# Issuing k^T v of two pairs of heads in one run, from the third batch on

## The chip, the cores and the metric

The kernel runs on one core of a Trainium2 chip. Its time is the device time of that core in microseconds (us), the median of several executions. Engines are written as in the profile: PE is TensorE's matmuls, PEld its weight loads, DVE VectorE, ACT ScalarE, POOL GpSimd, SP the engine that issues the transfers.

## The reference

```python
def _attn_ref(q, k, v, g_norm):            # (8, 8, 576, 64): batch, heads, sequence, head size
    kv = np.einsum('bhsd,bhse->bhde', k, v)
    out = np.einsum('bhsd,bhde->bhse', q, kv)
    rms = np.sqrt(np.mean(out * out, axis=-1, keepdims=True) + 1e-06)
    return out / rms * g_norm
def _moe_ref(x, w_gate, w_val, w_out):     # x: (4608, 512), w_gate and w_val: (512, 1536)
    gate = 1.0 / (1.0 + np.exp(-(x @ w_gate)))
    return gate * (x @ w_val) @ w_out
```

Linear attention without a softmax, normalised per head, and behind it a gated feed-forward layer over 4608 rows (casts, and the reshaping between the two, are left out above). The kernel computes in fp32; the weights come in 8 bytes an element and are converted in the start-up. The feed-forward layer is most of the work.

## The kernel before

The rows are handled in chunks of 512. The first two batches of attention are computed up front. The feed-forward layers of the first rows are done by *plain* matmuls, the rest by seven products of blocks in place of eight (p1 to p7 below). From the third batch on attention is a filler: each pair of heads is a list of steps, and one step goes out at each *slot*, a place between matmuls of the feed-forward layers. The steps of a pair are (cut; the 12 calls of `matmul` below show in the trace as 24 instructions, each of which I call a pass):

```python
def kv_mm():        # k^T v: 24 passes on TensorE, in two halves of the output's partitions
    d["kv"] = ps = at_ps("kv")
    for j in range(NJ):
        js = slice(HD * j, HD * j + HD)
        for e in range(2):
            nc.tensor.matmul(ps[HD * e:HD * e + HD, 0, 0:HD], pairs[n]["k"][:, e, js], pairs[n]["v"][:, e, js],
                             start=(j == 0), stop=(j == NJ - 1))
def kv_out():       # VectorE copies the two 64 x 64 blocks out
    ...
# q_mm transposes of q, q_out ScalarE copy to qT, u_mm q k^T v, u_square ScalarE, u_sum VectorE,
# u_root ScalarE, u_norm VectorE (L268, L270), x_mm transposes, x_out ScalarE copy (L288)
    return [kv_mm, kv_out, q_mm, q_out, u_mm, u_square, u_sum, u_root, u_norm, x_mm, x_out]
```

All four results on PSUM, where matmuls put their results (k^T v, transposed q, u, transposed x) take the same single buffer, "at":

```python
def at_ps(kind):
    return psum_at.tile([P, 2, 512], FP32, tag="at", name="at")
```

A block of the first layer on a chunk has seven pairs of products, each with one slot behind it; the sums of `h_sums` follow at its end:

```python
for i, (p, r) in enumerate(zip(one[0], two[0])):   # p1, p6, p2, p7, p5, p4, p3
    p()
    r()
    slot()
    ...
one[1]()
two[1]()
h_sums(c, f)
```

Six such blocks (slots 0 to 41) and a second layer with 28 more slots make one steady batch of 123.4 us.

Of the kernel before, what the change touches and what calls it, by code (L numbers as in the profile page):

```python
# [10 lines left out]
FP32 = mybir.dt.float32  # L11
# [12 lines left out]
def kernel(  # L24
# [13 lines left out]
    B, H, S, HD = q.shape  # L38
# [3 lines left out]
    NHP = H // 2  # L42
    NJ = 6
    NP = S // NJ
# [9 lines left out]
    sb = ctx.enter_context(tc.tile_pool(name="sb", bufs=2))  # L54
# [6 lines left out]
    first = first_ctx.__enter__()  # L61


    NE = 2 * NHP
    pairs = {n: {} for n in range(B * NHP)}

    def ahead(n):
        return (n + 4,) if n + 4 < NE else (NE,) if n + 1 == NE else () if n < NE else (n + 1,)

    def load_kv(n):  # L70
        if n >= B * NHP:
            return
        b, h0 = n // NHP, 2 * (n % NHP)
        for name, src in (("k", k), ("v", v)):
            t = (first if n < NE else sb).tile([NP, 2, NJ * HD], FP32, tag=name, name=name, bufs=4 if n < NE else 1)
            nc.sync.dma_start(out=t, in_=src[b, h0:h0 + 2].rearrange("h (p j) d -> p h (j d)", j=NJ))
            pairs[n][name] = t

    def load_q(n):
        if n >= B * NHP:  # L80
            return
        b, h0 = n // NHP, 2 * (n % NHP)
        t = (first if n < NE else sb).tile([NP, NJ, 2, HD], FP32, tag="q", name="q", bufs=4 if n < NE else 1)
        for e in range(2):
            nc.sync.dma_start(out=t[:, :, e, :], in_=q[b, h0 + e].rearrange("(p j) d -> p j d", j=NJ))
        pairs[n]["q"] = t
# [98 lines left out]
    for n in range(4):  # L185
        load_kv(n)
        load_q(n)
        if n == 0:
            load_next_unit()
# [18 lines left out]
    def chunk(c):  # L208
        if c not in xT:
            xT[c] = sb.tile([P, NMT, G], FP32, tag="xT", name="xT", bufs=3)  # L210
        return xT[c]

    def attention(n, at_ps):

        b, m = divmod(n, NHP)
        d = {}

        def kv_mm():
# [7 lines that stand above are left out]
        def kv_out():  # L226
            for e in range(2):
                es = slice(HD * e, HD * e + HD)
                nc.vector.tensor_copy(out=kvs[n % 2][es, es], in_=d["kv"][es, 0, 0:HD])
            for i in ahead(n):  # L230
                load_kv(i)

        def q_mm():
            d["q"] = ps = at_ps("q")
            for j in range(NJ):
                c0 = NP * (j % JH)
                nc.tensor.transpose(ps[:, j // JH, c0:c0 + NP], pairs[n]["q"][:, j].rearrange("p e d -> p (e d)"),  # L237
                                    ident[0:NP, 0:NP])

        def q_out():  # L240
            d["qT"] = sb.tile([P, 2, JH * NP], FP32, tag="qT", name="qT")
            nc.scalar.copy(out=d["qT"], in_=d["q"][:, :, 0:JH * NP])
            for i in ahead(n):
                load_q(i)

        def u_mm():

            ps = at_ps("u")
            d["u"] = ps[0:NP, :, 0:JH * P]
            for j in range(NJ):  # L250
                c0 = P * (j % JH)
                nc.tensor.matmul(ps[0:NP, j // JH, c0:c0 + P], d["qT"][:, j // JH, NP * (j % JH):NP * (j % JH) + NP],  # L252
                                 kvs[n % 2], start=True, stop=True)

        def u_square():
            d["sq"] = sb.tile([NP, 2, JH * P], FP32, tag="sq", name="sq")
            nc.scalar.activation(out=d["sq"], in_=d["u"], func=AF.Square)

        def u_sum():
            d["ms"] = sb.tile([NP, 2, 2 * JH], FP32, tag="ms", name="ms")  # L260
            nc.vector.tensor_reduce(out=d["ms"].rearrange("p i n -> p (i n)"),  # L261
                                    in_=d["sq"].rearrange("p i (n d) -> p (i n) d", d=HD), axis=AX.X, op=ALU.add)

        def u_root():
            nc.scalar.activation(out=d["ms"], in_=d["ms"], func=AF.Sqrt, bias=eps[0:NP], scale=1.0 / HD)

        def u_norm():
            nc.vector.reciprocal(d["ms"], d["ms"])  # L268
            d["xn"] = d["sq"]
            nc.vector.tensor_tensor(out=d["xn"].rearrange("p i (n d) -> p i n d", d=HD),  # L270
                                    in0=d["u"].rearrange("p i (n d) -> p i n d", d=HD),
                                    in1=d["ms"].unsqueeze(3).to_broadcast([NP, 2, 2 * JH, HD]), op=ALU.mult)

        def x_mm():
            d["x"] = ps = at_ps("x")
            for j in range(NJ):
                c0 = NP * (j % JH)
                nc.tensor.transpose(ps[:, j // JH, c0:c0 + NP], d["xn"][:, j // JH, P * (j % JH):P * (j % JH) + P],  # L278
                                    ident[0:NP, 0:NP])

        def x_out():

            s0 = 0
            while s0 < S:
                c, o = divmod(S * b + s0, G)
                i, r = divmod(s0, S // 2)
                n_ = min(G - o, S // 2 - r)
                nc.scalar.activation(out=chunk(c)[:, m, o:o + n_], in_=d["x"][:, i, r:r + n_], func=AF.Copy, scale=g_col)  # L288
                s0 += n_

        return [kv_mm, kv_out, q_mm, q_out, u_mm, u_square, u_sum, u_root, u_norm, x_mm, x_out]


    fill = deque()
# [3 lines left out]
            fill.popleft()()  # L298

    def feed(b, at_ps):  # L300
        for n in range(NHP * b, NHP * b + NHP):
            steps = attention(n, at_ps)

            fill.extend(steps[:-2] + [lambda: None] * 2 + steps[-2:])

    def flush():
        while fill:
# [27 lines left out]
    def at_ps(kind):  # L335
        return psum_at.tile([P, 2, 512], FP32, tag="at", name="at")
# [51 lines left out]
    late = deque()  # L388
# [230 lines left out]
    t2w[1] = b12  # L619
    tt(out=t2w[3], in0=b22, in1=b12, op=ALU.subtract)  # L620
    feed(2, at_ps)
    second_layer(0)
    for n in (1, 2, 3, 4):
# [19 lines left out]
    for c in range(2, NG):  # L643
        if c + 1 < B:
            feed(c + 1, at_ps)
        first_layer_fast(c)
        sums_of(c + 1)
        second_layer_fast(c)
        flush()
# [30 lines left out]
```

## Time and profile before

| | before |
|---|---|
| time, median of 3 | 1146.07 us (1144.22 to 1146.63) |
| profiled span | 1143.9 us |
| PE busy | 1118.9 us, 98% |
| chain that ended last | PE 93% |
| first plain matmul of the feed-forward layer starts | 45.80 us |
| from there to the first k^T v run of the steady part | 261.41 us |
| a steady batch | 123.38 us, five of them |

I call what lies ahead of the first plain matmul the start-up, the stretch from there to the first k^T v run of the steady part the mixed part (plain matmuls, the third batch's attention as filler), and a steady batch what lies from one batch's first k^T v run to the next batch's. In the view of the waits of the kernel before (who waited, at which line, for whom: us in total, times, longest), the following are all those of PE that lie behind the start-up; the first is five waits, one in each steady batch, and the last is again one a batch:

```profile
PE mm L507 <- DVE gv L519: 2.4, 5, 0.5
PE at L278 <- DVE sq L270: 2.2, 2, 1.6
...
PE at L223 <- ACT xT L288: 0.9, 5, 0.2
```

The idle time in this view begins where the matmul before ends by the profile's model; by starts the losses are larger, which is how the prediction counts them. The totals by window of one steady batch (from its start to the next; busy us and number of instructions of PE, PEld, DVE, ACT, POOL, then granted clock, transfers' share and GB/s):

```profile
305.00:428.38 123.38, 122.73 (x698) 107.43 (x697) 58.30 (x130) 35.25 (x71) 33.86 (x48) 1.00 0.15 38
```

PE is idle 0.65 us of 123.38, no other engine is busy half of the time (PEld is TensorE too). There is no large wait to win; anything that helps has to shorten or close up PE's own sequence.

### The profile page before, as it was taken

What the parts mean: (1) busy time and instruction counts of PE and PEld (TensorE: products, weight loads), DVE (VectorE), ACT (ScalarE), POOL (GpSimd) and SP (SyncE); (2) the same over time, 40 slices, a digit from 0 to 9 for tenths busy, and PEclk for the clock granted to TensorE, in tenths of its full rate; (3) what the DMA queues carried; (4) which work ended last, traced back from release to release, by engine and by line L of the source; (5) the groups of instructions that cost most, each with busy time, mean ns of one, the idle gap of its engine ahead of it and who ended that gap; (6) DMA issues with size and microseconds to landing.
All of it is one profiled execution on the core that took longest, in us unless ns stands there. A gap on an engine that the chain in (4) does not pass through costs nothing.

```text
span 1143.9 us, 14818 instructions
## 1 busy us (share of the span) xinstructions
PE 1118.9 (98%) x5712; PEld 891.6 (78%) x5712; DVE 583.7 (51%) x1121; ACT 296.2 (26%) x571; POOL 241.6 (21%) x342
## 2 busy tenths in 40 slices
PE   5899999999999999999999999999999999999998
PEld 4644444547888888888888888888888888888887
DVE  4699995054155525563365425552556246615641
ACT  3622221223133303331233213330333112101110
POOL 0000001000034303340143103430343025404420
PEclk9999999999999999999999999999999999999999
DMA  9843430211211111111111121111110000000001
GB/s 226 202 146 118 141 110 26 56 49 32 63 37 32 32 28 41 40 45 30 50 32 32 41 59 32 32 32 31 42 49 11 19 19 1 1 19 19 1 1 37
DMA packets 71589, 57.58 MB, mean 50 GB/s; under 512 B 40800, under 2 KB 65376, under 8 KB 71520
## 3 DMA queue, kind: packets, MB, share of 16 engines
q1 hardware_dynamic: 71360, 56.64, 18.5%
q8 instruction: 46, 0.75, 0.3%
q14 instruction: 23, 0.19, 0.1%
q10 hardware_dynamic: 160, 0.00, 0.0%
HBM read 47.19 MB, written 9.44 MB: 50 GB/s over the span
## 4 chain that ended last, share of the span: by engine, by line
PE 93%; DMA 3%; DVE 2%; ACT 1%; issue 1%; SPq 0%; DVEq 0%; ACTq 0%
PE mm L507 44%; PE mm L587 25%; PE two L378 10%; PE mm L363 4%; PE at L378 3%; DMA q<-in_q_dram 3%; PE at L252 3%; PE at L223 2%; PE at L278 1%; PE at L237 1%; PE mm L378 1%; ACT xT L288 0%; DVE sq L270 0%; DVE ms L261 0%; DVE sg L535 0%
## 5 line engine op out<-in xcount | busy, mean ns | idle before, releaser
L493 POOL TENSOR_TENSOR tw<-gv 128x256 f32<-128x256 f32 x168 | 120.3, 726 | 851.4 <-PE mm L507 661.6
L507 PE MATMUL mm<-xT,tw 128*128 128x256 f32 x672 | 160.1, 381 | 2.4 <-DVE gv L519 2.4
L507 PE MATMUL mm<-sx,tw 128*128 128x256 f32 x672 | 159.6, 380 | 0.0
L507 PE MATMUL mm<-xT,gv 128*128 128x256 f32 x672 | 159.4, 380 | 0.0
L507 PEld LDWEIGHTS mm<-xT,tw 128*128 128x128 f32 x672 | 124.9, 190 | 20.1 <-issue 4.2
L507 PEld LDWEIGHTS mm<-xT,gv 128*128 128x128 f32 x672 | 126.9, 190 | 17.2
L507 PEld LDWEIGHTS mm<-sx,tw 128*128 128x128 f32 x672 | 126.1, 190 | 16.7
L493 POOL TENSOR_TENSOR tw<-gv,tw 128x256 f32<-128x256 f32 x168 | 125.7, 769 | 0.0
L378 PE MATMUL two<-xT,gv 128*128 128x512 f32 x256 | 111.1, 593 | 0.5 <-DVE sq L270 0.5
L378 PEld LDWEIGHTS two<-xT,gv 128*128 128x128 f32 x256 | 48.4, 190 | 60.4 <-issue 60.2
L587 PE MATMUL mm<-w,s 128*128 128x256 f32 x384 | 89.1, 379 | 0.0
L587 PE MATMUL mm<-w,gv 128*128 128x256 f32 x384 | 88.3, 379 | 0.0
L587 PE MATMUL mm<-t2w,gv 128*128 128x256 f32 x384 | 88.1, 379 | 0.0
L536 ACT ACTIVATE sg<-sg 128x256 f32<-128x256 f32 x84 | 35.0, 416 | 187.9 <-DVE sg L535 187.3
L527 DVE TENSOR_TENSOR gv<-mm,sg 128x256 f32<-128x256 f32 x84 | 35.7, 424 | 88.9 <-PE mm L507 88.9
L587 PEld LDWEIGHTS mm<-t2w,gv 128*128 128x128 f32 x384 | 73.0, 190 | 9.9
L587 PEld LDWEIGHTS mm<-w,s 128*128 128x128 f32 x384 | 72.6, 190 | 9.7
L587 PEld LDWEIGHTS mm<-w,gv 128*128 128x128 f32 x384 | 72.5, 190 | 9.6
L507 PE MATMUL mm<-sx,gv 128*128 128x256 f32 x336 | 79.9, 381 | 0.0
L507 PEld LDWEIGHTS mm<-sx,gv 128*128 128x128 f32 x336 | 63.4, 190 | 8.8
L514 ACT COPY sg<-mm 128x256 f32<-128x256 f32 x84 | 31.3, 372 | 146.1 <-PE mm L507 146.1
L543 DVE TENSOR_TENSOR gv<-gv,sg 128x512 f32<-128x512 f32 x84 | 68.9, 859 | 0.2
(94 smaller groups left out, 1194.3 us busy)
## 6 DMA issues: line engine op xcount, KB each, us to landing
k<-in_k_dram SPq DMA_DIRECT2D x32, 288.0 KB, 3.3
v<-in_v_dram SPq DMA_DIRECT2D x32, 288.0 KB, 3.9
q<-in_q_dram SPq DMA_DIRECT2D x64, 144.0 KB, 3.1
st<-in_moe_w_gate_dram SPq DMA_DIRECT2D x12, 512.0 KB, 3.7
st<-in_moe_w_val_dram SPq DMA_DIRECT2D x12, 512.0 KB, 4.8
st<-in_moe_w_out_dram SPq DMA_DIRECT2D x12, 512.0 KB, 4.1
out_dram<-sg SPq DMA_DIRECT2D x24, 192.0 KB, 2.3
out_dram<-sg SPq DMA_DIRECT2D x24, 128.0 KB, 2.3
```

The costliest lines, as they stand in the source:

```text
L223: nc.tensor.matmul(ps[HD * e:HD * e + HD, 0, 0:HD], pairs[n]["k"][:, e, js], pairs[n]["v"][:, e, js], start=(j == 0), stop=(j == NJ - 1))
L237: nc.tensor.transpose(ps[:, j // JH, c0:c0 + NP], pairs[n]["q"][:, j].rearrange("p e d -> p (e d)"), ident[0:NP, 0:NP])
L252: nc.tensor.matmul(ps[0:NP, j // JH, c0:c0 + P], d["qT"][:, j // JH, NP * (j % JH):NP * (j % JH) + NP], kvs[n % 2], start=True, stop=True)
L363: nc.tensor.matmul(ps, gv[c, f][:, P * t:P * t + P], w["wo", f], start=(f == 0), stop=(f == NFT - 1))
L378: nc.tensor.matmul(self.ps[i], w[("wg", "wv")[i], self.f][:, m, :], xT[self.c][:, m, :], start=(m == 0), stop=(m == NMT - 1), skip_group_c ...
L493: nc.gpsimd.tensor_tensor(out=tw[f, i], in0=b[in0], in1=b[in1] if isinstance(in1, tuple) else tw[f, in1], op=ALU.subtract)
L507: nc.tensor.matmul(ps, wt[:, m, :], xs[:, m, :], start=(new and m == 0), stop=(m == NK - 1), skip_group_check=True)
L514: nc.scalar.copy(out=d["sg"][:, h2], in_=pa)
L527: tt(out=d["h"][:, h2], in0=pb, in1=d["sg"][:, h2], op=ALU.add)
L536: nc.scalar.activation(out=d["sg"][:, h2], in_=d["sg"][:, h2], func=AF.Sigmoid)
L543: tt(out=d["h"], in0=d["h"], in1=d["sg"], op=ALU.mult)
L587: nc.tensor.matmul(ps, hs(f), ws[:, f, :], start=(new and f == 0), stop=(f == NF2 - 1), skip_group_check=True)
```

## The change

Its intent: k^T v of two pairs of heads goes out as one run of 48 passes in place of two of 24, so that TensorE goes into and out of this kind of matmul half as often. Both results share one "at" buffer, in neighbouring columns. As both pairs' k and v must be there at once, their load buffers go from one to two, and are loaded two pairs ahead. The rest of each pair's steps follows, so every later step moves to another slot.

```diff
-    def ahead(n):
-        return (n + 4,) if n + 4 < NE else (NE,) if n + 1 == NE else () if n < NE else (n + 1,)
+    def ahead(n, late):
+        return (n + 4,) if n + 4 < NE else (n + late,) if n + late >= NE else ()
...   (load_kv: bufs=4 if n < NE else 1 becomes ... else 2; kv_out loads ahead(n, 2), q_out ahead(n, 1))
     def feed(b, at_ps):
-        for n in range(NHP * b, NHP * b + NHP):
-            steps = attention(n, at_ps)
-
-            fill.extend(steps[:-2] + [lambda: None] * 2 + steps[-2:])
+        for n in range(NHP * b, NHP * b + NHP, 2):
+            both = []
+
+            def tile_of(i, both=both):
+                def ps(kind):
+                    if kind != "kv":
+                        return at_ps(kind)
+                    if not both:
+                        both.append(at_ps(kind))
+                    return both[0][:, :, HD * i:HD * i + HD]
+                return ps
+
+            one, two_ = (attention(n + i, tile_of(i)) for i in range(2))
+
+            def kv_of_both(one=one, two_=two_):
+                one[0]()
+                two_[0]()
+
+            fill.extend([kv_of_both, one[1], two_[1]])
+            for steps in (one, two_):
+
+                fill.extend(steps[2:-2] + [lambda: None] * 2 + steps[-2:])
```

More of the change, by code (lines that the diff above doesn't have):

```diff
@@ L74, in load_kv @@
         for name, src in (("k", k), ("v", v)):
-            t = (first if n < NE else sb).tile([NP, 2, NJ * HD], FP32, tag=name, name=name, bufs=4 if n < NE else 1)
+            t = (first if n < NE else sb).tile([NP, 2, NJ * HD], FP32, tag=name, name=name, bufs=4 if n < NE else 2)
             nc.sync.dma_start(out=t, in_=src[b, h0:h0 + 2].rearrange("h (p j) d -> p h (j d)", j=NJ))
@@ L229, in kv_out @@
                 nc.vector.tensor_copy(out=kvs[n % 2][es, es], in_=d["kv"][es, 0, 0:HD])
-            for i in ahead(n):
+            for i in ahead(n, 2):
                 load_kv(i)
@@ L242, in q_out @@
             nc.scalar.copy(out=d["qT"], in_=d["q"][:, :, 0:JH * NP])
-            for i in ahead(n):
+            for i in ahead(n, 1):
                 load_q(i)
```

## The prediction

> **What bounds the kernel now.** I read the page's first and fourth parts, then the matmul timeline of one steady batch, then the full timeline around each gap in it.
>
> ```profile
> PE 1118.9 (98%) x5712; PEld 891.6 (78%) x5712; DVE 583.7 (51%) x1121; ACT 296.2 (26%) x571; POOL 241.6 (21%) x342
> ...
> PE 93%; DMA 3%; DVE 2%; ACT 1%; issue 1%; SPq 0%; DVEq 0%; ACTq 0%
> ```
>
> TensorE is busy 98% of the span and is 93% of the chain that ended last, so the end moves only by what is taken from, or added to, TensorE's own sequence. From 269 us the sequence repeats every 123.4 us (the k^T v run of a batch's first pair starts at 307.21, 430.59, 553.97, 677.34, 800.72): five batches with attention work mixed in, then one chunk without it. So I asked what one k^T v run (L223) costs there:
>
> ```profile
> 305.39 1.89 PE L507 MATMUL mm<-xT,gv 128*128 128x256 f32 x8
> 307.21 0.92 PE L223 MATMUL at<-v,k 96*64 96x64 f32 x24
> 308.06 1.99 PE L507 MATMUL mm<-sx,tw 128*128 128x256 f32 x8
> 309.89 1.89 PE L507 MATMUL mm<-xT,gv 128*128 128x256 f32 x8
> ...
> 320.36 1.89 PE L507 MATMUL mm<-xT,gv 128*128 128x256 f32 x8
> 322.09 1.89 PE L507 MATMUL mm<-sx,tw 128*128 128x256 f32 x8
> ```
>
> Starts are what counts; ends are modelled. Undisturbed, a block of eight L507 passes starts 1.727 us after the one before (322.09 - 320.36 = 1.73). With the run between, the third block starts 4.50 us after the first, so the run costs 4.50 - 2 x 1.727 = 1.046 us. The starts of the single instructions split it: 0.093 before its first pass, 0.697 from first to last start, 0.151 to the next L507, 0.104 lost behind that one. Inside, passes go in pairs (one for each half of the output's partitions), 7 ns apart, the next pair 52 ns on: 58.5 ns a pair, 0.70 us for 12 pairs. About 0.34 us of each run is therefore the price of going in and coming out.
>
> Next, the gaps that are no run. Per steady batch there are two, both on TensorE's path:
>
> ```profile
> 331.91 0.42 ACT L536 ACTIVATE sg<-sg 128x256 f32<-128x256 f32 x1 [0.45 <-DVE sg L535]
> 332.23 1.02 ACT L288 ACTIVATE xT<-at,g_col 128x288 f32<-128x288 f32 x3
> 333.31 0.92 PE L223 MATMUL at<-v,k 96*64 96x64 f32 x24 [0.17 <-ACT xT L288]
> ```
> ```profile
> 351.99 0.42 DVE L576 TENSOR_TENSOR s<-gv,s 128x256 f32<-128x256 f32 x1
> 352.33 0.21 DVE L268 RECIPROCAL ms<-ms 96x12 f32<-96x12 f32 x1
> 352.57 0.95 DVE L270 TENSOR_TENSOR sq<-at,ms 96x768 f32<-96x768 f32 x1
> 353.45 0.74 DVE L519 TENSOR_TENSOR gv<-mm,sg 128x256 f32<-128x256 f32 x2
> 354.01 1.97 PE L507 MATMUL mm<-xT,tw 128*128 128x256 f32 x8 [0.47 <-DVE gv L519]
> ```
>
> First: the second pair's k^T v needs the one "at" buffer, which ScalarE frees with L288, queued behind two sigmoids (L536). That run starts 0.334 us after its turn in place of 0.093: 0.241 lost. Second: VectorE does the normalisation of the second pair (L268, L270) just after the four sums of a block and before L519, and TensorE cannot overwrite its PSUM bank before L519 has read it. By single starts this is 0.638 plus a slower restart of 0.046: 0.684 lost. The first mixed batch, among the plain blocks, has two more, which the chain shows as VectorE:
>
> ```profile
> 255.85 0.69 PE L278 MATMUL at<-ident,sq 96*128 96x96 f32 x6 [1.65 <-DVE sq L270]
> ...
> 267.48 0.95 DVE L270 TENSOR_TENSOR sq<-at,ms 96x768 f32<-96x768 f32 x1
> 268.43 0.60 ACT L383 ACTIVATE sg<-mm 128x512 f32<-128x512 f32 x1
> 268.58 0.69 PE L278 MATMUL at<-ident,sq 96*128 96x96 f32 x6 [0.55 <-DVE sq L270]
> ```
>
> By starts they cost 1.81 and 0.71 us.
>
> **What the Trainium skill says.** "TensorEngine Tiling (Array Packing)", section "Key Properties", says that changing the tiling mode, not just the tile, drains TensorE. k^T v writes 64 columns to two halves of the output, the rest uses all 128; the trace agrees that a price is paid at both ends of the run (0.093; 0.151 where a pair starts 0.052 after the last; 0.104). "TensorE: Matmul & The Clock Gate", Part 2, step 1 says that weight loads are pulled ahead of matmuls in flight. The trace agrees for L507, whose load starts 0.21 us before its matmul (331.04, 331.25), but at the k^T v run both start at 333.31. "Trace Analysis", section "Tensor Engine Instruction", says that ScalarE and VectorE are strict FIFOs; the two gaps above are such queues: L519's matmul result was ready, and it stood behind L270.
>
> **The change part by part.** The instructions of the built kernel, engine by engine, confirm the order that I work out here.
>
> Merging: batches 2 to 7 have four k^T v runs of 24 passes each, 24 runs, which become 12 of 48. A double run costs 1.046 + 12 x 0.0585 = 1.748, two singles 2.092: 0.344 saved, 12 times, 4.1 us. The second half waits for its own two transfers in mid-run; they land long before (k and v take some 3 to 4 us, and are issued many us ahead), but its wait instructions (51 ns) may make a bubble. I allow 0.05 a merge, 0.5 us in all.
>
> Shifted steps: the work goes out one step per slot, and a slot follows each pair of products, seven to a block of the first layer. A pair took 13 slots; two now take 25 (3 + 2 x 11), four 50 in place of 52. Slots counted from 0:
> - The output copy L288 before the second pair's next use of "at" moves from slot 12 (sixth of its block, behind the sigmoids) to 13, after which the next user is a transpose at 14. Those of pairs one to three are now at 13, 24 and 38, none behind sigmoids with a user one slot later. The 0.241 goes.
> - The second pair's normalisation moves from slot 21 (first of a block, behind the sums) to 20, where the third pair's sits at 34 in both kernels: last slot of a block, with its transposes three slots later (23; 37), so that TensorE has about 0.5 us more to do before it needs L519. At 34 there is no gap today. The 0.684 goes.
> - The first pair's sum of squares (0.94 us) moves from slot 6 to 7, from ahead of the block's sums to behind them. VectorE does the same total before L519; today L519's first half ends at 324.97 there and its matmul starts at 325.54, so it keeps some 0.4 us. No gap.
> - The last pair's u matmuls move to slot 41, one slot behind their qT copy, which is behind two sigmoids. By today's times: copy from 332.23 to 332.87 on the analogous slot, matmul due at 332.98. Just enough; I charge 0.05.
>
> A steady batch saves 2 x 0.344 + 0.241 + 0.684 - 0.05 = 1.56 us, five of them 7.8 us.
>
> First mixed batch: the 1.81 gap ends when VectorE has done 10 us of queued sums, which start after the k^T v copies (243.27). The double run starts earlier but is longer, and two pairs of copies stand ahead: by the durations they start within 0.1 us of today. So the first merge and most of what comes before is swallowed. After that gap nothing but matmuls: no k^T v run (1.05 saved), and normalisation two slots (1.72 us) earlier, so the 0.71 gap goes. Together about 1.8 us.
>
> Loads: the second k and v buffer brings 576 KB forward to about 40 us, ahead of the fourth weight unit in the queue. That unit is converted only after 66 us; a delay of 2 us is hidden.
>
> Sum: 7.8 + 1.8 - 0.5 = 9.1 us.
>
> **Rivals.** (1) Only the merge counts, because new gaps replace the two that go: the slots move for every step, and VectorE has just 0.2 to 0.4 us of slack before L519. Against it: each critical position has a twin in the kernel before that runs free. It would give 4 us less the swallowed first merges: about 1142. (2) The merge saves nothing: the price is per pair or comes from waiting for the transfers, and reappears in mid-run. For it: the second half has waits of its own. Against it: the runs' price shows at their ends, and is the same in all steady ones but the late one. Then only the gaps count: 5 x 0.88 + 1.8, about 1140. (3) TensorE's whole stream shortens but another engine holds it: VectorE is at 51%, ScalarE 26%; only locally possible, as in (1). (4) Slower: the double run holds "at" longer and pushes the transposes into waits (two VectorE copies, 0.45 us each, must end first). A transpose now follows two slots after the first copy, and slot to slot is 1.73 us; it would need to go wrong in every batch by over 2 us to matter.
>
> **Range and chances.** 1146.07 - 9.1 = 1137.0. If a gap of 0.3 to 0.7 us reappears in each batch, 1138.5 to 1140.5; if the bubble is nil and the copies fit, 1136. Three runs of before spread over 2.4 us. So 1134.0 to 1141.0. Two per cent is 22.9 us, more than twice everything in the list: faster by over 2% gets 0.01, slower by over 2% 0.005.
>
> **What would show it.** In the profile after: L223 in twelve runs of 48 passes in place of 24 of 24, each 1.4 us from first to last start; the batch's period at 121.8 us in place of 123.4; no wait of TensorE for L288 and none of 0.47 for VectorE's product sum (L519 by the old numbering); the last transposes before the second fast layer without a wait; the period of L507 unchanged. Wrong would be: a hole in the middle of the 48 passes of 0.3 us, a wait of the u matmuls for the qT copy over 0.3 us, or a new wait for that product sum at another block.

## The result, and the profile after

The changed kernel takes 1134.64 us (1134.08 to 1135.97, five runs), the kernel before on the same occasion 1145.30 (1144.22 to 1146.63, five runs). The ratio is 0.9908, with a 95% interval of 0.9894 to 0.9922. Ratios here are the mean time of one kernel's runs over that of the other's of the same rounds, so not quite the ratio of the medians. This is a gain of some 0.9%, inside the 2% that counts as the same, and 1134.64 lies inside the predicted range of 1134.0 to 1141.0, near its lower end.

The profiled spans differ by 10.0 us, and the differences of starts add up to it: the start-up is the same (45.82 us), the mixed part after it goes from 261.41 to 259.60 (1.81 less), and a steady batch from 123.38 to 121.74 (1.64 less, five times 8.2). Lines of the changed file are 19 higher behind the diff: L526 is the old L507, L538 the old L519.

The page of the kernel after, busy time and the chain by engine:

```profile
PE 1113.2 (98%) x5712; PEld 892.0 (79%) x5712; DVE 582.1 (51%) x1121; ACT 296.9 (26%) x571; POOL 239.5 (21%) x342
...
PE 94%; DMA 3%; DVE 2%; SPq 0%; issue 0%; ACT 0%; DVEq 0%
```

The same number of matmuls, 5.7 us less of busy time. The timeline of PE at the first steady batch:

```profile
303.60 1.89 PE L526 MATMUL mm<-xT,gv 128*128 128x256 f32 x8
305.42 1.62 PE L223 MATMUL at<-v,k 96*64 96x64 f32 x48
306.96 1.99 PE L526 MATMUL mm<-sx,tw 128*128 128x256 f32 x8
308.80 1.89 PE L526 MATMUL mm<-xT,gv 128*128 128x256 f32 x8
```

The third block starts 5.20 us after the first, so the double run costs 5.20 - 2 x 1.727 = 1.75 us. Two single ones cost 2.09. By single starts: 0.093 ahead, 1.397 from first to last pass, 0.151 and 0.104 behind. The ends are those of a single run within 1 ns, and there is no hole between pass 24 and 25: starts are 7 and 52 ns apart in turn all through, but for 100 ns ahead of the second pair, as in a single run.

The two places where the steady batch used to wait, in the full timeline of the kernel after (start, duration, then the idle time before and its releaser in brackets where there was any):

```profile
330.29 0.42 ACT L555 ACTIVATE sg<-sg 128x256 f32<-128x256 f32 x1 [0.45 <-DVE sg L554]
330.61 1.03 ACT L288 ACTIVATE xT<-at,g_col 128x288 f32<-128x288 f32 x3
...
333.61 0.66 PE L237 MATMUL at<-ident,q 96*128 96x96 f32 x6
...
347.06 0.95 DVE L270 TENSOR_TENSOR sq<-at,ms 96x768 f32<-96x768 f32 x1
...
350.73 0.75 DVE L538 TENSOR_TENSOR gv<-mm,sg 128x256 f32<-128x256 f32 x2
350.99 0.66 PE L278 MATMUL at<-ident,sq 96*128 96x96 f32 x6
351.48 1.92 PE L526 MATMUL mm<-xT,tw 128*128 128x256 f32 x8
```

The output copy L288 is still behind the sigmoids, but it ends at 331.64, two us before the next user of "at". The normalisation L270 is now ahead of the block's sums, and PE spends the time until L538 on transposes that it owes anyway; its next product has no bracket. The steady batch as a window:

```profile
303.60:425.34 121.74, 121.74 (x698) 107.44 (x697) 57.93 (x130) 35.41 (x71) 33.42 (x48) 1.00 0.16 39
```

PE is busy for the whole of it. One wait is left behind the start-up, in the mixed part:

```profile
255.84 0.69 PE L278 MATMUL at<-ident,sq 96*128 96x96 f32 x6 [1.25 <-DVE sq L270]
...
266.81 0.66 PE L278 MATMUL at<-ident,sq 96*128 96x96 f32 x6
```

The third pair's transposes start at nearly the same time as before (255.85; 0.04 earlier counted from the first plain matmul), though everything ahead of them got shorter; the fourth pair's no longer wait.

### The profile page after: what moved, and what is told of

The parts are those of the page before. It is cut to its first block, busy times and chain, and to the rows that moved or that the text cites. A ratio compares the mean times of both kernels' runs of the same rounds, so it can differ in the third digit from the quotient of the medians.

```text
span 1133.9 us, 14824 instructions
## 1 busy us (share of the span) xinstructions
PE 1113.2 (98%) x5712; PEld 892.0 (79%) x5712; DVE 582.1 (51%) x1121; ACT 296.9 (26%) x571; POOL 239.5 (21%) x342
## 4 chain that ended last, share of the span: by engine, by line
PE 94%; DMA 3%; DVE 2%; SPq 0%; issue 0%; ACT 0%; DVEq 0%
PE mm L526 45%; PE mm L606 26%; PE two L397 10%; PE mm L382 4%; PE at L397 3%; DMA q<-in_q_dram 3%; PE at L252 3%; PE at L223 2%; PE at L278 1%; PE at L237 1%; PE mm L397 1%; DVE sq L270 0%; DVE ms L261 0%; SPq L85 0%; SPq L76 0%; DVE w L648 0%
## 5 line engine op out<-in xcount | busy, mean ns | idle before, releaser
L526 PE MATMUL mm<-xT,tw 128*128 128x256 f32 x672 | 159.7, 380 | 0.0
L526 PE MATMUL mm<-sx,tw 128*128 128x256 f32 x672 | 159.7, 380 | 0.0
L526 PE MATMUL mm<-xT,gv 128*128 128x256 f32 x672 | 158.8, 379 | 0.0
L526 PEld LDWEIGHTS mm<-xT,gv 128*128 128x128 f32 x672 | 127.7, 190 | 17.4
L526 PEld LDWEIGHTS mm<-sx,tw 128*128 128x128 f32 x672 | 126.1, 190 | 16.7
L526 PEld LDWEIGHTS mm<-xT,tw 128*128 128x128 f32 x672 | 125.3, 190 | 16.1
L526 PE MATMUL mm<-sx,gv 128*128 128x256 f32 x336 | 79.5, 379 | 0.0
L526 PEld LDWEIGHTS mm<-sx,gv 128*128 128x128 f32 x336 | 63.1, 190 | 8.2
```

Source lines behind the costliest of these rows:

```text
L526: nc.tensor.matmul(ps, wt[:, m, :], xs[:, m, :], start=(new and m == 0), stop=(m == NK - 1), skip_group_check=True)
```

## The experiments

The gain has two possible parents, the merge and the moved slots, which the change does together. Four experiments take them apart, a fifth looks at why a run has a price at its ends, a sixth tries the last wait, and the changed kernel ran once more beside them. All gave the right result. As the start-up varied (the plain matmuls began anywhere from 44.20 to 46.78 us), I compare three quantities of each trace: where the plain matmuls start, the length of the mixed part from there to the first k^T v run of the steady part, and the steady batch.

| run | span | plain start | mixed part | steady batch | time, median | ratio to before, 95% |
|---|---|---|---|---|---|---|
| before | 1143.9 | 45.80 | 261.41 | 123.38 | | |
| changed | 1133.9 | 45.82 | 259.60 | 121.74 | 1134.64 | 0.9908 (0.9894 to 0.9922) |
| e1_merged_old_slots | 1137.7 | 44.53 | 261.19 | 122.44 | 1141.72 | 0.9965 (0.9951 to 0.9980) |
| e2_split_new_slots | 1140.8 | 46.04 | 262.85 | 122.43 | 1142.57 | 0.9974 (0.9959 to 0.9989) |
| e3_slot_moved_no_merge | 1139.7 | 46.37 | 261.42 | 122.42 | 1141.20 | 0.9960 (0.9943 to 0.9976) |
| e4_transposes_one_later | 1140.8 | 45.57 | 261.42 | 122.80 | 1142.51 | 0.9973 (0.9958 to 0.9988) |
| e5_full_width_kv | 1143.7 | 44.21 | 261.60 | 123.61 | 1146.52 | 1.0014 (0.9997 to 1.0030) |
| e6_sums_later | 1130.8 | 44.20 | 258.16 | 121.74 | 1133.78 | 0.9900 (0.9885 to 0.9915) |
| e7_changed_again | 1134.8 | 46.78 | 259.60 | 121.74 | 1135.82 | 0.9920 (0.9906 to 0.9935) |

The kernel before had medians of 1145.15 us beside the first four experiments and 1145.12 beside the last three. A span agrees with its expectation only as far as the start-up does: the full-width run, for one, met its 1143.5 with a start-up 1.6 us shorter than that of the changed kernel, and like for like would be at 1145.3.

**The merge alone (e1_merged_old_slots).** Edit, against the changed kernel:

```diff
-            fill.extend([kv_of_both, one[1], two_[1]])
-            for steps in (one, two_):
-                fill.extend(steps[2:-2] + [lambda: None] * 2 + steps[-2:])
+            def out_of_both(one=one, two_=two_):
+                one[1]()
+                two_[1]()
+            for steps, first_two in ((one, [kv_of_both, out_of_both]), (two_, [lambda: None] * 2)):
+                fill.extend(first_two + steps[2:-2] + [lambda: None] * 2 + steps[-2:])
```

> The k^T v of two pairs merged as in the changed kernel, but every other step left in its old slot (two idle slots stand where the second pair's own k^T v and its copy stood). My theory (the merge saves 0.345 us each by itself; the wait for L288 goes because no k^T v run follows that output copy any more; the wait behind the normalisation of the second pair stays, because its slot stays): the steady batch goes from 123.38 to 123.38 - 2 x 0.345 - 0.241 = 122.45 us, and still has one TensorE wait of about 0.64 us for VectorE per batch. In the first mixed batch VectorE's queue starts about 0.9 us later, which eats most of the 1.05 us there. Profiled span about 1139, time about 4.8 us under before. Rival A (the merge itself saves nothing, the gain came from moved slots): only 5 x 0.241 goes, span 1142.5 to 1143. Rival B (the merge removes both waits): span about 1135.5.

Measured: a steady batch of 122.44 us, and the wait behind the normalisation where it was, as PE's timeline of this run shows (L540 is the old L519):

```profile
351.93 1.97 PE L528 MATMUL mm<-xT,tw 128*128 128x256 f32 x8 [0.47 <-DVE gv L540]
```

The span is 1137.7 with a start-up 1.3 us shorter than before, so 1139.0 like for like, as expected. (The time is 0.35% under before, or 4.0 us by the means, where 4.8 was expected.) Both rivals fall: the merge does save, and it does not remove the wait for VectorE.

**The new slots alone (e2_split_new_slots).** Edit, against the changed kernel:

```diff
-            fill.extend([kv_of_both, one[1], two_[1]])
+            def out_of_both(one=one, two_=two_):
+                one[1]()
+                two_[1]()
+            fill.extend([one[0], two_[0], out_of_both])
```

> The changed kernel with the merge undone and all other slots kept: the two k^T v runs stand in two neighbouring slots, a pair of products between them, and both copies in the third slot. My theory: each of the 12 merges is given back, 0.345 us, and nothing else in the steady batches: period 121.73 + 0.69 = 122.42 us, no wait for L288, none behind the normalisation. In the first mixed batch the queue on VectorE starts about 1 us later. Span about 1133.9 + 10 x 0.345 + 1 = 1138.4. Rival A (all the gain is slots): span stays at 1134. Rival C (a run on its own costs more than its ends, for example because its copies come later): span over 1140.

Measured: a steady batch of 122.43, so 0.69 for two merges, 0.345 each, and no wait in it. Its PE timeline shows the two runs that stand where the one of 48 stood:

```profile
308.89 0.92 PE L223 MATMUL at<-v,k 96*64 96x64 f32 x24
309.74 2.00 PE L530 MATMUL mm<-sx,tw 128*128 128x256 f32 x8
311.66 0.92 PE L223 MATMUL at<-v,k 96*64 96x64 f32 x24
```

The span missed its expectation by 2.4 us, and all of that beyond 0.2 of start-up is in the mixed part: 262.85 is 3.25 over the changed kernel, and I had expected about 1. VectorE's queue started 1.56 us later, not 1 (the third of its large sums starts 202.58 us after the plain matmuls here, 201.02 in the changed kernel). And after the wait of 2.28 us that this made for PE, the array ran at half its clock for a while. The windows of this run (same columns as above):

```profile
257.00:259.00 2.00, 1.38 (x7) 1.14 (x8) 0.47 (x1) 0.42 (x2) 0.00 (x0) 0.73 0.00 0
259.00:262.00 3.00, 3.00 (x10) 1.33 (x9) 0.00 (x0) 0.62 (x3) 0.00 (x0) 0.61 0.00 0
262.00:266.00 4.00, 4.00 (x22) 2.54 (x21) 0.69 (x1) 3.13 (x4) 0.00 (x0) 1.00 0.32 74
```

The granted clock falls to 0.61 in the second window. The trace's clock record has it at 0.5 from 257.93 for 3.41 us, which costs 1.71; 1.56 + 1.71 = 3.27 accounts for the 3.25. In e1_merged_old_slots a wait of the same 2.27 us passed without it. In each trace the clock changes only on a grid of 3.41 us. Here the wait (255.50 to 257.62 by the modelled ends) lies whole in one interval of that grid, 254.52 to 257.93, in which PE is busy 38%, and the clock falls at its end. In e1_merged_old_slots the wait (253.30 to 255.41) is cut by the grid at 254.85, and PE is busy 55% and 84% in the two intervals. This would fit a count of PE's work in each interval, but these runs don't show that it is the cause.

**One slot moved, no merge (e3_slot_moved_no_merge).** Edit, against the kernel before (L513 is the old L507 here and in the next run):

```diff
-            fill.extend(steps[:-2] + [lambda: None] * 2 + steps[-2:])
+            idle = [lambda: None]
+            if n % NHP == 0:
+                fill.extend(steps[:-2] + idle + steps[-2:])
+            elif n % NHP == 1:
+                fill.extend(steps[:-2] + idle * 2 + steps[-2:] + idle)
+            else:
+                fill.extend(steps[:-2] + idle * 2 + steps[-2:])
```

> The kernel before with one idle slot taken from the first pair of each batch and put behind the second pair, so that the second pair's steps come one slot earlier (its normalisation at slot 20, its last transposes at 23, the first pair's output copy at 11); no merge. My theory: both waits of the steady batch go, 5 x (0.241 + 0.684) = 4.6 us, and nothing else changes: period 123.38 - 0.925 = 122.46 us, span about 1139.3. Rival B (the waits went because of the fewer runs): span stays at 1143.9, or just one of the two waits goes.

Measured: a steady batch of 122.42 us, mixed part unchanged, both waits gone. So more than half of the steady gain was to be had without the merge, by moving one idle slot. The timeline of PE at the place of the old wait:

```profile
351.98 1.89 PE L513 MATMUL mm<-xT,gv 128*128 128x256 f32 x8
353.71 0.66 PE L278 MATMUL at<-ident,sq 96*128 96x96 f32 x6
354.21 1.92 PE L513 MATMUL mm<-xT,tw 128*128 128x256 f32 x8
```

**The transposes one slot later (e4_transposes_one_later).** Edit, against the run just told:

```diff
-                fill.extend(steps[:-2] + idle * 2 + steps[-2:] + idle)
+                fill.extend(steps[:-2] + idle * 3 + steps[-2:])
```

> As the run with the idle slot moved, but a third idle slot ahead of the second pair's last transposes, which then stand at slot 24, behind the block's fourth pair of products in place of ahead of it. My theory (these transposes are what gives VectorE the time for its product sum behind the normalisation): a wait of about 0.32 us plus a restart of 0.05 comes back in each of five batches: period about 122.83, span about 1141.1. Rival: the place of the transposes does not matter, the same as with the idle slot moved, about 1139.3.

Measured: 122.80 us, 0.38 more. The product that waits for VectorE now comes straight after the one before, and late:

```profile
351.18 1.89 PE L513 MATMUL mm<-xT,gv 128*128 128x256 f32 x8
353.21 1.96 PE L513 MATMUL mm<-xT,tw 128*128 128x256 f32 x8
```

These starts are 2.03 us apart in place of 1.73: a wait of 0.30, with 0.075 more for the second pass behind it. The transposes between the two were what hid it. The other part, 0.34 of the 0.713 that the old wait cost, stays saved: it belongs to the earlier place of the normalisation.

**Full width (e5_full_width_kv).** Edit, against the changed kernel:

```diff
+                if n >= NE:
+                    nc.tensor.matmul(ps[:, 0, 0:P], pairs[n]["k"][:, j].rearrange("p e d -> p (e d)"),
+                                     pairs[n]["v"][:, j].rearrange("p e d -> p (e d)"),
+                                     start=(j == 0), stop=(j == NJ - 1))
+                    continue
...   (k and v loaded per head, as q is; the copies take the two diagonal blocks; 128 columns a pair in "at")
```

> The changed kernel, but from the third batch on k^T v is computed at full width: both heads of a pair in one matmul of 128 x 128 columns, of which the diagonal blocks are used (right result; k and v are loaded in the layout of q, in 144 KB pieces). Twice the work, but no change of the array's tiling. A pass then takes 109 ns as in the u matmuls, 24 passes a double run. My theory (what a k^T v run costs at its ends comes with the change of tiling): the ends vanish: the first pass one period (0.216) after the last of the product, no loss behind the run: 24 x 0.109 = 2.62 us a double run in place of 1.745, 0.87 more; period about 121.73 + 1.75 = 123.5, span about 1143.5. Rival D (the ends come with the small matmuls' own waits for transfers and buffers): the ends stay at about 0.35 us, 2.96 a double run, span about 1147.5.

Measured: the ends are gone. PE's timeline (L229 and L537 here):

```profile
304.08 1.89 PE L537 MATMUL mm<-xT,gv 128*128 128x256 f32 x8
305.81 2.84 PE L229 MATMUL at<-v,k 96*128 96x128 f32 x24
308.49 1.89 PE L537 MATMUL mm<-sx,tw 128*128 128x256 f32 x8
310.22 1.89 PE L537 MATMUL mm<-xT,gv 128*128 128x256 f32 x8
```

The first pass starts 1.73 us after the block before it, on time, and the blocks behind are 1.73 apart again: by single starts nothing is lost ahead of the run and 0.004 behind it. It waits for transfers and for the same buffer as the narrow one does. One more thing differs at the ends: here the run's first weight load starts 0.215 us ahead of its matmul (305.593, 305.808), while at a narrow run the first load and the first matmul start within 2 ns of each other (307.211 and 307.213 in the kernel before), and so do those of the product behind it (308.060, 308.061). The run takes 2.68 us for 24 passes of 112 ns, a little over the 109 assumed; hence 123.61 in place of 123.5. Rival D would have given about 124.2. So the price sits with the narrow, two-tile form of these matmuls, not with their waits. Width and tiling changed together here, so which of the two sets it is not taken apart. As a version it is no use: it does twice the array's work to save the ends.

**The sums later (e6_sums_later), and the changed kernel again (e7_changed_again).** Edit, against the changed kernel:

```diff
             tt(out=t2w[4], in0=b21, in1=t2w[2], op=ALU.subtract)
+        elif f == NFT - 2:
             for i in range(NF2 - 3):
                 h_sums(1, i)
```

> The changed kernel with one more move: in the first mixed batch the twelve small sums of the first three blocks (5 us of VectorE) are issued after the second plain block in place of the first. My theory (the third pair's transposes wait 1.42 us because its sum of squares stands behind 10 us of sums in VectorE's queue): that wait goes altogether, and nothing comes back: span 1133.9 - 1.4 = 1132.5, time about 1133.2. Rival: the wait only moves, to the second layer's products that need those sums: no change.

> The changed kernel as it is, for comparison in the same rounds: span about 1132 to 1134, time about 1134.6. All theories say the same.

Measured: the mixed part falls from 259.60 to 258.16 us, 1.44 less, and no wait of PE is left in it. The timeline of the moved pair:

```profile
247.90 0.95 DVE L261 TENSOR_REDUCE ms<-sq 96x12 f32<-96x768 f32 x1 [0.91 <-ACT sq L257]
...
252.81 0.66 PE L278 MATMUL at<-ident,sq 96*128 96x96 f32 x6
```

The sum of squares (L261) no longer stands behind ten us of VectorE's other sums; it even waits for ScalarE. In the same rounds this kernel took 1133.78 us and the changed one 1135.82, with means in the ratio 0.9900 to 0.9920 against the kernel before. Its four times (1132.94 to 1134.16) all lie below the four of the changed kernel in these rounds (1135.12 to 1137.29), so it is the faster of the two there; how much of that is the step, the trace tells better (1.44 us), as the profiled start-ups differ by 2.58. Against the kernel before it is 1.0%, and the best version. The repeat has the mixed part and the steady batch of the changed kernel to 0.01 us; its span of 1134.8 and time missed their expectations (1132 to 1134, 1134.6) by about 1 us, which is its later start-up.

A merge of all four pairs of a batch was written too, but did not fit, and did not run. The changed kernel with its k and v buffers alone set to four doesn't build either: the loads of the start-up need 36 KB a partition where 32.66 KB are left.

## Why the prediction was right

- *TensorE's own sequence sets the end.* Right: PE is 94% of the chain after, and the steady batch has it busy for 121.74 of 121.74 us.
- *A merge saves 0.344.* Right: 0.345, from the ends in both traces, and from the 122.43 - 121.74 between split and merged. That the price belongs to the change of tiling was taken from a page and the place of the loss; the run at full width shows that it goes when neither width nor tiling changes. The prediction's example of a load not pulled ahead (333.31) is of the run that was late for its buffer; the undisturbed run at 307.21 is the better one, and shows the same.
- *A bubble in mid-run, 0.05 a merge.* Wrong, and harmless: none. 0.5 us of the sum was not spent.
- *Both steady waits go because slots move.* Right for the wait behind the normalisation: it stays with the merge alone and goes with the slot alone. The wait for L288 goes in either case: with the merge alone because the copy's next user comes later (L288 at 331.45, the user at 335.64), with the slot alone because the copy goes ahead of the sigmoids (328.55, 331.63). The prediction named only the move of slots, and took the copy of the changed kernel not to be behind the sigmoids. It is, but they now end 1.1 us after the start of the transposes that it copies (329.63), not 3.3, so it is done in time. As this wait goes both ways, the gains of merge alone (0.93) and slot alone (0.95) add up to 0.24 more than that of both (1.64).
- *0.684 for the wait behind the normalisation.* Mis-sized by 0.03: I took a restart of 0.046 where the second start behind the wait is 0.075 late, and nothing is to be set against it. 0.638 + 0.075 = 0.713. With it a batch sums to 2 x 0.345 + 0.241 + 0.713 = 1.644, as measured. This restart shows again in the run with the late transposes.
- *VectorE's sums in another order leave 0.4 us of slack; transposes hide the rest.* Right: no wait there, and moving the transposes by one slot brought back 0.38 a batch, where 0.37 was expected.
- *0.05 for the u matmuls behind their copy.* Not spent: they start on time in every batch.
- *Mixed part 1.8.* Right: 1.81. The third pair's transposes start where they did, within 0.04 us of the mixed part, so that the savings ahead of them are swallowed.
- *Loads.* Right as far as the end goes: the plain matmuls start at 45.82 against 45.80 and have no new wait. (A small delay would not show in a start-up that varies by 2.6 us.) k and v take 4.8 and 5.3 us to land (median) in place of 3.3 and 3.9, two pairs being issued together.
- *Sum.* 9.1 predicted, 10.0 in the spans. The missing 0.9 is the 0.5 for the bubble, 0.25 for the copies and 5 x 0.03 for the restart. The timed gain was 0.92% in one set of rounds and 0.80% in the other; both contain the 10.0 us of 1143.9, or 0.87%. Of the 2.4 us between the point forecast of 1137.0 and the 1134.64, another 0.8 is the base: the forecast started from 1146.07, and the five runs of the kernel before have a median of 1145.30. That the result lies inside the range is in part luck: it is 0.6 us from the lower end, and the start-up alone moved by more than that between runs.

Of the rivals, (1) and (2) fall by the two-by-two of merge and slots: 123.38 with neither, 122.44 and 122.43 with one (122.42 by the other slot move), 121.74 with both. (3) and (4) did not show.

## What to carry to other kernels

When one engine is busy all the time, read single starts instead of idle times: a kind of instruction that comes in short runs can cost half as much again as its passes, at its ends, and gathering two runs into one pays that once in place of twice. A change that moves a list of filler steps also moves every other wait; check for each queue what stands ahead of what at each new place, and test the moved places apart from the idea itself, because half of the gain in a steady batch needed only one idle slot elsewhere. And a wait of the busy engine for another that is no sooner done swallows what is saved ahead of it, so look for the last one left and ask what its releaser was doing.

## What the Trainium skill lacked or had wrong

- "TensorEngine Tiling (Array Packing)", section "Key Properties", says that a change of tiling mode drains TensorE but gives no price. Here the narrow runs lose 0.345 us each among back-to-back fp32 products: 0.093 us ahead, the rest behind and at the second pair of passes; at full width 0.004. That all of it is the drain is not shown.
- "TensorE: Matmul & The Clock Gate", Part 1, has the clock fall to half after an idle window of about 3.4 us. In the run with split k^T v a wait of 2.28 us was followed by 3.41 us at half clock, while one of 2.27 us in another run was not; PE was idle for 2.12 us of the 3.41 at whose end the clock fell.
- None of the pages cited here has the second late start after a wait: after PE stood for a semaphore in mid-stream, the second pass came 0.075 us late as well (0.638 and 0.301 us of wait, the same 0.075).
- Nor do they say how much a start-up bound by transfers varies: the same sequence of loads let the plain matmuls start between 44.20 and 46.78 us, more than some of the effects measured here.
